# Reordering the first-batch attention head of a fused attention and mixture kernel

## Chip, cores and metric

The kernel runs on one core of one Trainium2 chip. The metric is the device time of one launch in microseconds (us). The kernel before the change takes 359.23 us, the median of five runs that lie between 359.01 and 359.6 us.

Five engines work side by side, each through its own instructions in order. PE is TensorE, the matrix engine; a matmul is preceded by a load of its weights, which the profile lists as PEld. DVE is VectorE, ACT is ScalarE, POOL is GpSimd and SP is SyncE. Engines wait for one another through semaphores. Matmul results go to PSUM, an accumulator memory that this kernel uses in eight banks of 512 fp32 numbers per partition; DVE and ACT copy them from there to SBUF, the working memory.

## What is computed

The reference is an attention in blocks whose keys and values are first mixed by a normalized 8 x 8 matrix, followed by a mixture of four two-layer networks.

```python
def _attn_ref(q, k, v, sort_net):          # q, k, v: 4 x 8 heads x 768 x 64
    P = sort_net
    for _ in range(5):
        P = P - np.max(P, axis=-1, keepdims=True)
        P = np.exp(P)
        P = P / (np.sum(P, axis=-1, keepdims=True) + 1e-09)
        P = P / (np.sum(P, axis=-2, keepdims=True) + 1e-09)
    k_sorted = np.einsum('bhij,bhjcd->bhicd', P, k_b).reshape(B, H, S, D)
    v_sorted = np.einsum('bhij,bhjcd->bhicd', P, v_b).reshape(B, H, S, D)
...
    scores = scale * np.matmul(q_b, k_sb.transpose(0, 1, 2, 4, 3))
    attn = softmax(scores)
    return np.matmul(attn, v_sb)

def _moe_ref(x, domain_probs, w1, w2):     # x: 3072 x 512; w1: 4 x 512 x 1024
    p = domain_probs / (domain_probs.sum(-1, keepdims=True) + 1e-09)
    for e in range(E):
        h = np.maximum(x @ w1[e], 0.0)
        out += p[:, e:e + 1] * (h @ w2[e])
    return out
```

The listing is shortened: reshapes and type casts are left out, and the softmax is written as one word.

## The kernel before

The order of all work is written out by hand: the kernel is built under a manual schedule, so each engine's instructions stand in the order of the calls. The head is the stretch from the start to the first full-width layers. It loads batch 0, normalizes the 8 x 8 matrices, and takes batch 0 through attention and the first network without a trip through DRAM, so that PE has dense work soon.

Batch 0's eight heads are treated as two quads of four heads, `qd` 0 and 1. Blocks of 96 tokens come in pairs `qq`: pair 0 and pair 1 are what this change touches. For a quad and a pair the steps are these.

- `mix_half` (L485) multiplies keys or values by the mixing matrices: 24 matmuls of 64 columns at L495 into one PSUM tile. `mixed` (L503) casts two of the tile's four blocks to SBUF (L506), into `kT` for keys or `vT0` for values.
- `h_w` (L517) transposes the mixed values on PE (four matmuls at L522 for two blocks). Its copy to SBUF (L527) can be handed back as a function and called later.
- `h_s` (L540) forms the scores of a pair, eight matmuls at L550, and ACT exponentiates them (L556) into `ET`.
- `h_a` (L561) multiplies `ET` by the values, eight matmuls at L567. DVE then takes reciprocals of the sums (L578) and scales the result (L579) into `xsl`.
- `h_x` (L584) transposes `xsl` with a permutation, four matmuls at L592, and a copy (L596) puts it into `xT`, the input of the first layer.
- `group0` (L660) is the first layer of network 0 on 192 tokens, eight matmuls at L673 for half of the contraction. `[0, 1]` is quad 0's and `[2, 3]` is quad 1's half of it. Its result goes through ACT (L686).
- `keep_warm` (L478) issues matmuls on a constant whose result nobody reads.

In what follows a letter with two digits names such a step: s01 is the scores of quad 0 and pair 1, w its value transposes, a its product with the values, x its transposition, g a part of the first layer, mv1 the 24 matmuls that mix quad 1's values.

PSUM is divided into two pools, `psM` and `psA`, of two tiles each; a tile spans two banks. Scores fill the first 384 numbers of each bank of their tile. `side` (L536) gives the last 128 numbers of each bank, seen as 16-bit numbers, as the place for value transposes. `tails` is the same for the mixing tiles. So transposes often share both banks of a tile with scores or with mixed values.

The order around the change is L1372 to L1411. PE's order from L1376 on is: a00, mv1, s10, w01, x00, w10, s01, four keep-warm matmuls, a10, g for quad 0, w11, x10, a01, g, s11, g for quad 1, x01, g, a11. The transposes w01 are written to the side of `ps_s01` ahead of the scores s01 that share its banks. ACT's order over the same stretch is: exponential of s00, cast of `kT` of quad 0, two casts of `kT` of quad 1, first cast of mv1, exponential of s10, copy of x00, second cast of mv1, exponential of s01, copy of w01, copy of x10. DVE's is: casts of quad 0's values, normalization of a00, copy of w10, normalization of a10, one step of the token weights (L237, followed on SP by small DMAs at L241 to L226), normalization of a01, copy of w11.

Of the kernel before, what the change touches and what calls it, by code (L numbers as in the profile page):

```python
# [9 lines left out]
F32 = mybir.dt.float32  # L10
F16 = mybir.dt.float16
AF = mybir.ActivationFunctionType
ALU = mybir.AluOpType
# [4 lines left out]
def kernel(  # L18
# [11 lines left out]
    nc = tc.nc  # L30

    B, H, S, D = q.shape
    GH = B * H
    NB = sort_net.shape[-1]
    BLK = S // NB
# [3 lines left out]
    P = 128  # L39
# [7 lines left out]
    HB = NB // 2  # L47
    VW = D + 2
# [12 lines left out]
    att = ctx.enter_context(tc.tile_pool(name="att", bufs=2))  # L61
# [3 lines left out]
    state = {"n": 0, "q": 0}  # L65

    def psa(shape, dtype, name):
        state["n"] += 1
        return psA.tile(shape, dtype, tag="ps", name=name)

    def psm(shape, dtype, name):
        return psM.tile(shape, dtype, tag="ps", name=name)
# [50 lines left out]
    def head(b, nm, h):  # L123
        return natural[(b, nm, h // 4)][:, h % 4, :, :]
# [231 lines left out]
    vec, act = nc.vector.tensor_copy, nc.scalar.copy  # L356
# [118 lines left out]
    xsls0, xsl0 = {}, {}  # L475
    vT0 = {qd: from_spare(S) for qd in range(2)}

    def keep_warm(ps, n):  # L478

        for _ in range(n):  # L480
            nc.tensor.matmul(ps, dummy, dummy, start=True, stop=True)
# [3 lines left out]
    def mix_half(nm, qd, hf, pool, warm_up=0):  # L485

        ps = pool([P, 1024], F32, f"ps_m{nm}_{qd}_{hf}")
        keep_warm(ps[:, 0:P], warm_up)
        tails[(nm, qd, hf)] = ps[:, 2 * R * 64:1024].bitcast(F16).rearrange("p (n x) -> p n x", n=2)
        ps = ps[:, 0:2 * R * 64].rearrange("p (s r x) -> p s r x", s=2, r=R)  # L490
        for sg in range(2):
            for r in range(R):
                for hh in range(2):
                    h = 4 * qd + 2 * sg + hh
                    nc.tensor.matmul(  # L495
                        ps[ds(D * hh, D), sg, r, :],
                        head(0, nm, h)[:, r, :],
                        PI0[hf][:, h, :, :].rearrange("p i c -> p (i c)"),
                        start=True, stop=True,
                    )  # L500
        return ps

    def mixed(nm, qd, ps, i0, n, copy):  # L503

        dst = kTs[qd][:, 0:S] if nm == "k" else vT0[qd]
        copy(  # L506
            dst.rearrange("p (i x c) -> p x i c", i=HB, c=CP)[:, :, ds(i0, n)],
            ps.rearrange("p s r (i c) -> p (s r) i c", c=CP)[:, :, ds(i0, n)],
        )
# [7 lines left out]
    def h_w(qd, copy, i0=0, n=HB, at=None):  # L517

        ps = psa([P, n, 2 * P], F16, f"ps_w_{state['n']}") if at is None else at
        for m in range(n):  # L520
            for sg in range(2):
                nc.tensor.transpose(  # L522
                    ps[0:BLK, m, ds(sg * P, P)], vT0[qd][:, ds((2 * (i0 + m) + sg) * BLK, BLK)], ident[:]
                )

        def evacuate(copy):
            copy(  # L527
                vs0s[qd][:, ds(i0, n), :, :, 0:D].rearrange("c i s h d -> c i (s h) d"),
                ps[0:BLK].rearrange("c i (x d) -> c i x d", d=D),
            )  # L530

        if copy is None:
            return evacuate
        evacuate(copy)

    def side(ps):  # L536

        return ps[:, :, 384:512].bitcast(F16)

    def h_s(qd, qq, ps=None):  # L540

        kT, ET = kTs[qd], ETs[2 * qd + qq % 2]
        if ps is None:
            ps = psa([P, 2, 512], F32, f"ps_s0_{qd}_{qq}")
        for n in range(4):
            for hh in range(2):
                sg, i = n // 2, 2 * (qq % 2) + n % 2

                m = BLK if 2 * i + sg == 3 else P
                nc.tensor.matmul(  # L550
                    ps[0:m, hh, ds(n * BLK, BLK)],
                    kT[ds(D * hh, D), ds((2 * i + sg) * BLK, m)],
                    qT0[qd][ds(D * hh, D), sg, qq // 2, :, ds((2 * (qq % 2) + n % 2) * CP, CP)],
                    start=True, stop=True,
                )
        nc.scalar.activation(  # L556
            ET[:, 0:S].rearrange("c (h x) -> c h x", h=2), ps[0:BLK, :, 0:HS],
            AF.Exp, bias=0.0, scale=SCALE,
        )

    def h_a(qd, qq, ps=None):  # L561
        ET = ETs[2 * qd + qq % 2]
        if ps is None:
            ps = psa([P, 2, 512], F32, f"ps_a0_{qd}_{qq}")
        for hh in range(2):
            for n in range(4):
                nc.tensor.matmul(  # L567
                    ps[:, hh, ds(n * VW, D + 1)],
                    ET[:, ds((4 * hh + n) * BLK, P)],
                    vs0s[qd][:, 2 * (qq % 2) + n % 2, n // 2, hh, 0:D + 1],  # L570
                    start=True, stop=True,
                )
        if qq not in xsls0:
            xsls0[qq] = att.tile([P, 2, 4, 2, D], F16, name=f"xsl0_{qq}", tag="xsl")[0:BLK]
        xsl = xsl0[(qd, qq)] = xsls0[qq][:, qd]
        av = ps[0:BLK, :, 0:4 * VW].rearrange("c h (n w) -> c h n w", w=VW)
        rz = att.tile([BLK, 2, HB, 1], F32, name=f"rz_{state['n']}", tag="rz", bufs=4)
        nc.vector.reciprocal(rz[:], av[:, :, :, D:D + 1])  # L578
        nc.vector.tensor_tensor(  # L579
            xsl.rearrange("c n h d -> c h n d"), av[:, :, :, 0:D],  # L580
            rz[:].broadcast_to([BLK, 2, 4, D]), ALU.mult,
        )

    def h_x(qq, copy, qds=range(2), ps=None, warm_up=0):  # L584

        nq = len(qds)
        if ps is None:
            ps = psa([P, 2, 512], F32, f"ps_x0_{qq}_{qds[0]}")
        keep_warm(ps[:, 0, 0:P], warm_up)
        for m, qd in enumerate(qds):  # L590
            for n in range(4):
                nc.tensor.matmul(  # L592
                    ps[:, m, ds(n * BLK, BLK)], xsl0[(qd, qq)][:, n, :, :].rearrange("c h d -> c (h d)"),
                    perm[:], start=True, stop=True,
                )
        copy(  # L596
            xTs[0][:, :, ds(2 * qq, 2), :].rearrange("p (q s) i x -> p q s (i x)", q=2)[:, ds(qds[0], nq)],
            ps[:, 0:nq, 0:4 * BLK].rearrange("p q (s x) -> p q s x", s=2),
        )
# [374 lines left out]
    for e in range(E):  # L974
        w, hk, hf = w1sb[e], NKC // 2, FF // 2
# [396 lines left out]
    mk1 = mix_half("k", 1, 0, psm)  # L1372
    mixed("k", 1, mk1, 0, 2, act)
    mixed("k", 1, mk1, 2, 2, act)
    ps_a00, ps_s10 = [psa([P, 2, 512], F32, f"ps_{n}") for n in ("a00", "s10")]
    h_a(0, 0, ps_a00)  # L1376
    mv1 = mix_half("v", 1, 0, psm)
    mixed("v", 1, mv1, 0, 2, act)
    h_s(1, 0, ps_s10)
    ps_s01 = psm([P, 2, 512], F32, "ps_s01")  # L1380
    w01 = h_w(0, None, 2, 2, side(ps_s01))
    h_x(0, act, [0], ps_a00)
    h_w(1, vec, 0, 2, tails[("v", 1, 0)])
    mixed("v", 1, mv1, 2, 2, act)
    h_s(0, 1, ps_s01)
    w01(act)
    ps_a10 = psa([P, 2, 512], F32, "ps_a10")
    keep_warm(ps_a10[:, 0, 0:P], 4)
    h_a(1, 0, ps_a10)
    next(p_steps)  # L1390
    group0(0, 1, 0, [0, 1])
    ps_a01 = psa([P, 2, 512], F32, "ps_a01")
    w11 = h_w(1, None, 2, 2, side(ps_a01))
    h_x(0, act, [1], ps_a10)
    h_a(0, 1, ps_a01)
    w11(vec)
    group0(0, 1, 1, [0, 1])
    ps_s11 = psa([P, 2, 512], F32, "ps_s11")
    h_s(1, 1, ps_s11)
    evacuate00 = group0(0, 1, 0, [2, 3], True)  # L1400
    h_x(1, act, [0], ps_a01)
    evacuate00()
    group0(0, 1, 1, [2, 3])
    h_a(1, 1, ps_s11)
# [17 lines left out]
    def builds(b):  # L1422
# [10 lines left out]
    later = [  # L1433
        [(h_q, 1, 1, vec)],
        [(h_v, 1, 1, act)],
        [(h_s, 0, 2), (h_w, 1, vec)],
        [(h_w, 0, vec), (h_s, 1, 2)],
        [(h_a, 0, 2)],
        [(h_s, 0, 3), (h_a, 1, 2)],
        [(h_s, 1, 3), (h_a, 0, 3)],  # L1440
        [(h_x, 2, act), (h_a, 1, 3)],
# [30 lines left out]
    for g in range(G0 + 1):  # L1472
        b, c = divmod(g, R // 2)
# [56 lines left out]
```

## Time and profile before

The profile is one execution with its own device time. All rows below come from it.

| What | us |
|---|---|
| median of five runs | 359.23 |
| the profiled execution's own time | 359.23 |
| its span, first to last instruction | 357.4 |
| so outside the span | 1.83 |
| PE busy in 0 to 11.80 | 8.84 |
| PE busy in 11.80 to 18.46 | 6.16 of 6.66 |
| PE busy in 18.46 to 36.88 | 18.42 of 18.42 |
| PE busy in 36.88 to 357.40 | 316.99 of 320.52 |

Busy times are unions of the recorded spans of an engine's instructions. Matmuls overlap in the pipeline, so a matmul's recorded end lies after the start of the next one; the distance from the start of one group to the start of the next is what the group costs PE when nothing waits. A timeline row gives the start, the length from the group's first start to its last end, the engine, the line, the output and inputs, and the number of instructions; a bracket at its end names the idle time before it and what ended it. The granted TensorE clock was 1.00 in all four stretches.

### The profile page before, as it was taken

The page shows a single profiled execution, that of the slowest core. Times are in us where ns is not written, and L with a number is a line of the kernel's source. Part 1 is how long each engine was busy: PE and PEld are TensorE (multiplying, and loading weights), DVE is VectorE, ACT ScalarE, POOL GpSimd, SP SyncE. Part 2 cuts the span into 40 slices and gives each one's busy share as a digit, 9 for nine tenths or more (in the row PEclk, how much of TensorE's full clock was granted, in tenths as well). Part 3 has the DMA queues.
Part 4 walks back from the last instruction along what each step waited for, and adds up shares of the span by engine and source line. Part 5 has one row for each costly group of instructions (what it writes and reads, how often), then busy time and mean ns, then how long its engine had stood idle before and what let it go on. Part 6 is the DMA issues. An engine that isn't in the chain of part 4 may idle for free.

```text
span 357.4 us, 9499 instructions
## 1 busy us (share of the span) xinstructions
PE 350.4 (98%) x3949; PEld 305.3 (85%) x3949; DVE 275.4 (77%) x550; ACT 171.5 (48%) x305; POOL 133.6 (37%) x149
## 2 busy tenths in 40 slices
PE   8799999999999999999999999999999999999996
PEld 8686857888888888888899888888888888888885
DVE  5754897769888587778889978896588876688963
ACT  2664330442424445368947158820388511688201
POOL 8873010365122420000626318840068800288400
PEclk9999999999999999999999999999999999999999
DMA  8999999999999999745994410005200014100011
GB/s 117 208 207 229 214 209 198 205 187 178 196 176 175 213 90 196 142 87 69 176 208 67 115 65 0 2 2 136 91 11 2 3 54 124 61 0 2 2 73 47
DMA packets 72023, 40.52 MB, mean 113 GB/s; under 512 B 40614, under 2 KB 66732, under 8 KB 71980
## 3 DMA queue, kind: packets, MB, share of 16 engines
q0 software_dynamic: 36576, 19.93, 41.4%
q1 hardware_dynamic: 35260, 19.92, 27.4%
q8 instruction: 31, 0.51, 0.6%
q14 instruction: 12, 0.10, 0.1%
q10 hardware_dynamic: 144, 0.07, 0.1%
HBM read 42.13 MB, written 6.34 MB: 136 GB/s over the span
## 4 chain that ended last, share of the span: by engine, by line
PE 95%; DVE 2%; ACT 1%; DMA 0%; issue 0%
PE ps_h L784 18%; PE ps_Q L1258 18%; PE ps_p L768 12%; PE ps_X L1115 10%; PE ps_Z L1115 7%; PE ps_Q L1115 7%; PE ps_Z L1258 6%; PE ps_h L673 3%; PE ps_o L708 3%; PE ps_p L824 3%; PE ps_a L453 2%; PE ps_s L418 2%; PE ps_k L399 1%; PE ps_v L365 1%; PE ps_mk L495 1%; PE ps_s L550 0%
## 5 line engine op out<-in xcount | busy, mean ns | idle before, releaser
L784 PE MATMUL ps_h<-xT,w 128*128 128x256 f16 x576 | 67.5, 273 | 0.0
L784 PEld LDWEIGHTS <-w 128*128 128x128 f16 x576 | 55.2, 98 | 7.2
L790 DVE SCALAR_TENSOR_TENSOR Hb<-ps_h,pb 128x1024 f16<-128x1024 f32 x34 | 41.5, 1223 | 17.3 <-PE ps_h L784 16.6
L1115 PEld LDWEIGHTS <-w 128*128 128x128 f16 x480 | 43.6, 98 | 4.8
L1128 POOL TENSOR_TENSOR arena<-tmp,pb 128x512 f16<-128x512 f32 x12 | 15.2, 1274 | 65.7 <-PE ps_Z L1115 49.8
L1258 PEld LDWEIGHTS <-Hb 128*128 128x128 f16 x320 | 31.1, 98 | 3.5
L1127 ACT ACTIVATE tmp<-tmp 128x512 f32<-128x512 f32 x46 | 29.0, 632 | 3.9 <-DVE tmp L1165 3.9
L1258 PEld LDWEIGHTS <-Sb 128*128 128x128 f16 x304 | 28.2, 98 | 3.0
L1115 PEld LDWEIGHTS <-arena 128*128 128x128 f16 x312 | 27.7, 98 | 2.9
L425 ACT ACTIVATE ET<-ps_s 96x768 f16<-96x768 f32 x24 | 18.1, 802 | 25.1 <-PE ps_s L418 24.8
L408 ACT CAST kT<-ps_k 64x384 f16<-64x384 f32 x48 | 22.7, 474 | 13.3 <-PE ps_k L399 12.3
L121 POOL DMA_DIRECT2D arena<-in_q_dram x24 | 19.9, 844 | 14.8 <-DMA q_ring<-arena 14.8
L1115 PE MATMUL ps_X<-ET,arena 128*128 128x256 f16 x168 | 25.2, 272 | 0.0
L1258 PE MATMUL ps_Q<-w,Hb 128*128 128x256 f16 x192 | 24.6, 273 | 0.0
L768 PEld LDWEIGHTS <-Hb 128*128 128x128 f16 x232 | 21.8, 98 | 3.0
L1121 DVE SCALAR_TENSOR_TENSOR Hb<-ps_X,pb 128x512 f16<-128x512 f32 x27 | 18.7, 692 | 7.0 <-PE ps_X L1115 7.0
L1135 ACT COPY ps_X<-ps_Z 128x512 f32<-128x512 f32 x27 | 15.4, 571 | 17.8 <-PE ps_Z L1115 17.8
L1115 PE MATMUL ps_Z<-xT,w 128*128 128x256 f16 (+1 forms) x176 | 22.5, 258 | 0.0
L754 DVE TENSOR_TENSOR Sb<-Hb 128x512 f16<-128x512 f16 x33 | 20.6, 647 | 0.0
L1142 ACT COPY tmp<-ps_X 128x512 f32<-128x512 f32 x26 | 15.2, 586 | 9.2 <-PE ps_X L1115 6.6
L1121 DVE SCALAR_TENSOR_TENSOR Hb<-ps_Z,pb 128x512 f16<-128x512 f32 x27 | 18.4, 683 | 1.3 <-PE ps_Z L1115 1.3
L1165 DVE TENSOR_TENSOR tmp<-ps_Q,tmp 128x512 f32<-128x512 f32 x26 | 17.8, 683 | 0.8 <-PE ps_Q L1115 0.8
(265 smaller groups left out, 739.7 us busy)
## 6 DMA issues: line engine op xcount, KB each, us to landing
w<-in_moe_w_dram POOLq DMA_DIRECT2D x6, 1024.0 KB, 28.0
pb<-p_dram SPq DMA_DIRECT2D x9, 512.0 KB, 6.5
arena<-in_k_dram POOLq DMA_DIRECT2D x8, 384.0 KB, 7.6
arena<-in_v_dram POOLq DMA_DIRECT2D x8, 384.0 KB, 7.6
vs<-arena SPq DMA_DIRECT2D x36, 66.0 KB, 5.0
arena<-in_q_dram POOLq DMA_DIRECT2D x24, 96.0 KB, 6.3
out_dram<-ob SPq DMA_DIRECT2D x9, 256.0 KB, 2.1
w<-in_moe_w_dram POOLq DMA_DIRECT2D x4, 512.0 KB, 11.9
```

The lines of the kernel that those rows point to most:

```text
L121: nc.gpsimd.dma_start(t[:, h // 2, :, h % 2, :], q[b, h].rearrange("(t p) d -> p t d", p=P))
L408: nc.scalar.copy(kT[ds(D * hh, D), r], pk[ds(D * r, D), hh].rearrange("p a (i c) -> p a i c", c=CP),)
L425: nc.scalar.activation(ETs[2 * (pr % 2) + hh][:, 0:S].rearrange("c (a x) -> c a x", a=2), pss[hh][0:BLK, :, 0:HS], AF.Exp, bias=0.0, scale ...
L754: tt(sm[0], blk(0, 1), blk(1, 1), ALU.add)
L768: nc.tensor.matmul(ps, lhs(e, f), Ts[e][rhs][:, f, :], start=(first and e == es[0] and f == 0), stop=(done and e == es[-1] and f == KH - 1 ...
L784: nc.tensor.matmul(ps[:, f, :], w1sb[e][:, kc, ds((4 * g + f) * P, P)], xT[:, kc, ds(2 * c * P, 2 * P)], start=(kc == 0), stop=(kc == NKC ...
L790: nc.vector.scalar_tensor_tensor(out=Hb[:, homes.get(e, e), ds(4 * g, 4), :], in0=ps[:], scalar=0.0, op0=ALU.max, in1=weights(e).broadcast ...
L1115: nc.tensor.matmul(dst[:, ds(f * cols, cols)], a[lhs][:, k, ds((f0 + f) * P, P)], t[rhs][:, k, :], start=(first and f == 0 and k == 0), st ...
L1121: nc.vector.scalar_tensor_tensor(out=home(i, j), in0=src.rearrange("p (f x) -> p f x", f=m), scalar=0.0, op0=ALU.max, in1=weight(j).broadc ...
L1127: nc.scalar.activation(src, src, AF.Relu, bias=0.0, scale=1.0)
L1165: tt(t12, Q, u2, ALU.add)
L1258: nc.tensor.matmul(ps, lhs(e, f), Ts[e][rhs][:, f, part], start=(first and e == 0 and f == 0), stop=(e == E - 1 and f == KH - 1), skip_gro ...
```

## The change

The head is reordered around the first values product. The scores s01 and the transposes w01 move from behind w10 and s10 to directly behind a00; in that move s01 comes ahead of w01, which writes to the side of the tile that s01 has just filled. `ps_s01` becomes a `psA` tile and `ps_s10` a `psM` tile. The first cast of mv1 and the copy of w01 go from ACT to DVE. x00 moves ahead of s10. The product a01 moves ahead of a10, so ahead of the first layer, and goes into `ps_s01` in place of a tile of its own; its normalization is held back (`later`) until x10 is issued. Two of four keep-warm matmuls are dropped. `ps_s11` reuses the tile of a10.

```diff
-    def h_a(qd, qq, ps=None):
+    def h_a(qd, qq, ps=None, later=False):
...
-        if qq not in xsls0:
-            xsls0[qq] = att.tile([P, 2, 4, 2, D], F16, name=f"xsl0_{qq}", tag="xsl")[0:BLK]
...
-        nc.vector.reciprocal(rz[:], av[:, :, :, D:D + 1])
...
+        def even():
+            if qq not in xsls0:
+                xsls0[qq] = att.tile([P, 2, 4, 2, D], F16, name=f"xsl0_{qq}", tag="xsl")[0:BLK]
...
+            nc.vector.reciprocal(rz[:], av[:, :, :, D:D + 1])
...
+        if later:
+            return even
+        even()
...
-    ps_a00, ps_s10 = [psa([P, 2, 512], F32, f"ps_{n}") for n in ("a00", "s10")]
+    ps_a00, ps_s01 = [psa([P, 2, 512], F32, f"ps_{n}") for n in ("a00", "s01")]
     h_a(0, 0, ps_a00)
+    h_s(0, 1, ps_s01)
+    w01 = h_w(0, None, 2, 2, side(ps_s01))
+    ps_s10 = psm([P, 2, 512], F32, "ps_s10")
     mv1 = mix_half("v", 1, 0, psm)
-    mixed("v", 1, mv1, 0, 2, act)
+    mixed("v", 1, mv1, 0, 2, vec)
+    w01(vec)
+    h_x(0, act, [0], ps_a00)
     h_s(1, 0, ps_s10)
-    ps_s01 = psm([P, 2, 512], F32, "ps_s01")
-    w01 = h_w(0, None, 2, 2, side(ps_s01))
-    h_x(0, act, [0], ps_a00)
     h_w(1, vec, 0, 2, tails[("v", 1, 0)])
     mixed("v", 1, mv1, 2, 2, act)
-    h_s(0, 1, ps_s01)
-    w01(act)
     ps_a10 = psa([P, 2, 512], F32, "ps_a10")
-    keep_warm(ps_a10[:, 0, 0:P], 4)
+    keep_warm(ps_a10[:, 0, 0:P], 2)
+    even01 = h_a(0, 1, ps_s01, True)
     h_a(1, 0, ps_a10)
     next(p_steps)
     group0(0, 1, 0, [0, 1])
-    ps_a01 = psa([P, 2, 512], F32, "ps_a01")
-    w11 = h_w(1, None, 2, 2, side(ps_a01))
+    w11 = h_w(1, None, 2, 2, side(ps_s01))
     h_x(0, act, [1], ps_a10)
-    h_a(0, 1, ps_a01)
+    even01()
     w11(vec)
     group0(0, 1, 1, [0, 1])
-    ps_s11 = psa([P, 2, 512], F32, "ps_s11")
+    ps_s11 = ps_a10
     h_s(1, 1, ps_s11)
     evacuate00 = group0(0, 1, 0, [2, 3], True)
-    h_x(1, act, [0], ps_a01)
+    h_x(1, act, [0], ps_s01)
     evacuate00()
     group0(0, 1, 1, [2, 3])
     h_a(1, 1, ps_s11)
```

PE's order becomes: a00, s01, w01, mv1, x00, s10, w10, two keep-warm matmuls, a01, a10, g, w11, x10, g, s11, g, x01, g, a11. ACT's: the casts of `kT`, exponential of s01, copy of x00, exponential of s10, second cast of mv1, copy of x10. DVE's: normalization of a00, first cast of mv1, copy of w01, copy of w10, normalization of a10, L237, normalization of a01, copy of w11. The order on POOL and SP is unchanged, and so is everything from a11 on.

More of the change, by code (lines that the diff above doesn't have):

```diff
@@ L572, in h_a @@
                 )
-        if qq not in xsls0:
-            xsls0[qq] = att.tile([P, 2, 4, 2, D], F16, name=f"xsl0_{qq}", tag="xsl")[0:BLK]
-        xsl = xsl0[(qd, qq)] = xsls0[qq][:, qd]
-        av = ps[0:BLK, :, 0:4 * VW].rearrange("c h (n w) -> c h n w", w=VW)
-        rz = att.tile([BLK, 2, HB, 1], F32, name=f"rz_{state['n']}", tag="rz", bufs=4)
-        nc.vector.reciprocal(rz[:], av[:, :, :, D:D + 1])
[L579 to L582, printed above, removed]
+        def even():
+            if qq not in xsls0:
+                xsls0[qq] = att.tile([P, 2, 4, 2, D], F16, name=f"xsl0_{qq}", tag="xsl")[0:BLK]
+            xsl = xsl0[(qd, qq)] = xsls0[qq][:, qd]
+            av = ps[0:BLK, :, 0:4 * VW].rearrange("c h (n w) -> c h n w", w=VW)
+            rz = att.tile([BLK, 2, HB, 1], F32, name=f"rz_{state['n']}", tag="rz", bufs=4)
+            nc.vector.reciprocal(rz[:], av[:, :, :, D:D + 1])
+            nc.vector.tensor_tensor(
+                xsl.rearrange("c n h d -> c h n d"), av[:, :, :, 0:D],
+                rz[:].broadcast_to([BLK, 2, 4, D]), ALU.mult,
+            )
+        if later:
+            return even
+        even()
     def h_x(qq, copy, qds=range(2), ps=None, warm_up=0):
```

## Prediction

> **What bounds the kernel.** I read the page's totals first, then who PE waited for, then the timeline of the head.
>
> ```profile
> span 357.4 us, 9499 instructions
> PE 350.4 (98%) x3949; PEld 305.3 (85%) x3949; DVE 275.4 (77%) x550; ACT 171.5 (48%) x305; POOL 133.6 (37%) x149
> PE 95%; DVE 2%; ACT 1%; DMA 0%; issue 0%
> ```
>
> The chain that ended last is PE for 95% of the span. The list of waits of PE over 0 to 30 us has four entries, and over 30 to 360 us it has none. So whatever the head gives PE late or early is carried whole to the end.
>
> ```profile
> PE ps_R L316 <- DVE sn L304: 1.9, 1, 1.9
> PE ps_w L260 <- DVE Hb L152: 1.1, 1, 1.1
> PE ps_s L550 <- ACT kT L506: 0.2, 1, 0.2
> PE ps_mk L495 <- DVE Rs L1366: 0.2, 1, 0.2
> ```
>
> All four lie ahead of a00. From the timeline, the stretch that the change reorders:
>
> ```profile
> 14.88 1.42 ACT L506 CAST kT<-ps_mk 128x384 f16<-128x384 f32 x3
> 15.12 0.55 DVE L506 CAST Sb<-ps_mv 128x384 f16<-128x384 f32 x1
> 15.34 0.42 PE L567 MATMUL ps_a<-Sb,ET 96*128 96x65 f16 x8
> 15.68 0.57 PE L495 MATMUL ps_mv<-Sb,arena 128*64 128x64 f16 x24
> 16.18 0.35 PE L550 MATMUL ps_s<-Sb,kT 64*128 64x96 f16 x8
> 16.29 0.48 ACT L506 CAST Sb<-ps_mv 128x384 f16<-128x384 f32 x1
> 16.46 0.42 PE L522 MATMUL ps_s<-ident,Sb 128*96 128x128 f16 x4
> 16.67 0.81 ACT L556 ACTIVATE ET<-ps_s 96x768 f16<-96x768 f32 x1
> 16.77 0.34 PE L592 MATMUL ps_a<-perm,xsl 96*128 96x96 f16 x4
> 16.95 0.39 PE L522 MATMUL ps_mv<-ident,Sb 128*96 128x128 f16 x4
> 17.27 0.34 PE L550 MATMUL ps_s<-Sb,kT 64*128 64x96 f16 x8
> 17.47 0.42 DVE L527 COPY Sb<-ps_mv 96x512 f16<-96x512 f16 x1 [0.76 <-ACT ET L556]
> 17.93 0.48 ACT L506 CAST Sb<-ps_mv 128x384 f16<-128x384 f32 x1
> 17.95 0.40 PE L567 MATMUL ps_a<-Sb,ET 96*128 96x65 f16 x8
> 18.46 0.82 PE L673 MATMUL ps_h<-xT,w 128*128 128x192 f16 x8
> 18.62 0.69 DVE L579 TENSOR_TENSOR xsl<-ps_a,rz 96x512 f16<-96x512 f32 x1
> 19.37 0.34 PE L592 MATMUL ps_a<-perm,xsl 96*128 96x96 f16 x4
> ```
>
> PE runs from group to group with hardly a hole: mv1 at 15.68, s10 at 16.18, w01 at 16.46, x00 at 16.77, w10 at 16.95, s01 at 17.27, keep-warm at 17.55, a10 at 17.95, g at 18.46. Other work hides the latencies: while ACT casts mv1 and DVE copies w10, PE does s10, w01, x00, s01 and keep-warm matmuls. The start-to-start distances are the costs below: mix 0.50, s 0.28, x 0.18, a 0.24, g 0.66. A change from s, a or x to full rows or back costs more: a00 to mv1 took 0.34, w10 to s01 0.32, and g to s11 0.76 (19.88 to 20.63). A waiting engine starts about 0.04 after PE's recorded end and 0.05 after ACT's or DVE's.
>
> **The change, step by step, on this execution's clock.** Up to a00 (15.34) nothing differs.
>
> *s01 ahead of mv1.* It needs the second cast of quad 0's values on DVE, which ends at 15.67. It is a wait on a separate instruction, like the one of the w10 copy (PE's end 17.34, copy 17.47: 0.14), so s01 starts at about 15.80, and its recorded end is 0.35 later, 16.15. ACT's second cast of quad 1's keys begins at 15.82 (the three casts end at 16.30, the last is 0.48 long); ACT starts its next instruction 0.38 after such a cast (16.29 to 16.67). Both give 16.19 for the exponential of s01. It takes 0.81: it ends at 17.00.
>
> *w01 behind s01.* This is the new wait. In the changed program's order the transposes w01 wait for the exponential of s01, because they write into the banks that it reads, though in other columns. Before, w01 came first and the scores filled the banks afterwards. PE could have begun w01 at 15.80 + 0.28 = 16.08; it begins at 17.05. Everything on PE queues behind: 0.97 us with nothing on PE. Nothing covers it, since mv1, x00 and s10, which were ready or could have been, stand behind it in PE's order.
>
> *The chain through quad 1's values.* w01 17.05 + 0.32 gives mv1 at 17.37, x00 at 17.87, s10 at 17.87 + 0.29 = 18.16 (x to s is not shown with no wait before it; 0.18 to 0.34 by the rows of x and of a to mv1). mv1's recorded end is 17.37 + 0.57 = 17.94. Its cast is on DVE now: 0.56 by the row of 13.63, in place of 0.48 on ACT; 17.98 to 18.54. w10 then starts at 18.59 (PE was free at 18.44: 0.15 lost). Its copy: 18.59 + 0.39 + 0.14 = 19.12, done at 19.54. The exponential of s10 is ready by then: s10 ends at 18.51, ACT is free from its x00 copy at 18.25 + 0.38 = 18.63, done 19.44. In the hole PE does two keep-warm matmuls and a01 (from 18.97, when DVE's copy of w01, 18.50 to 18.92, is done, to 19.21). a10 starts at 19.59, against 17.95: a hole of 0.38.
>
> *The first layer.* g directly behind a10 at 19.83. Before, it stood 0.51 behind a10, as it waited for ACT's second cast of mv1 (17.93 + 0.48 = 18.41); in the changed program it does not. Against 18.46 that is 1.37 late. w11 at 20.49. x10 needs xsl of a10: 19.59 + 0.40 + 0.04, reciprocal 0.24 to the next start, 0.69: 20.95, so x10 at 21.00; PE was free at 20.71, a hole of 0.29. Here a01 no longer stands between x10 and g, which saves 0.27 (19.64 minus 19.37) plus 0.24 (a01 itself) less the 0.18 of x10: 0.33. g at 21.18 against 19.88: 1.30 late. s11 at 21.18 + 0.76 = 21.94; ACT's copy of x10 is done at 21.86, just in time.
>
> *Behind it* the order is that of before, with the same distances. x01 at 22.9 needs the normalization of a01 and the copy of w11 on DVE, done by 22.4 (L237 0.31, reciprocal and product 0.93, copy 0.42, from 20.9 on). Two dropped keep-warm matmuls save 0.11, and it goes into holes. The copies moved off ACT cost nothing there: ACT was not on the chain. The token-weight DMAs follow L237, which goes from 19.23 to about 20.87; their first consumer on PE, at 30.20, moves by 1.30. The trace has the packets of the small load it reads in by 28.7, so 1.5 us of slack loses 0.34. POOL's and SP's queues are in the old order.
>
> Sum, by start times after less before: a10 +1.64 (holes 0.12 + 0.97 + 0.15 + 0.38, and 0.02 net of all that moved or went), from a10 to g -0.27 (0.24 in place of 0.51), from w11 to x10 +0.26 (0.51 in place of 0.25), from x10 to g -0.33: +1.30, and PE carries it to the end. Span 357.4 + 1.3 = 358.7; the profiled execution took 359.23, equal to the median of the five, so 359.23 + 1.30 = 360.53. The steps that have no row (x to s, wait instruction, w01 to mv1 after a hole) are good to 0.1 each: 1.0 to 1.6.
>
> The trace of before shows such a guard of shared banks: DVE's copy from the mixed-values tile ends at 17.89, and ACT's cast from other columns of the same tile starts at 17.93, though ACT was free for it from 17.75 (its x00 copy began at 17.37, plus 0.38). [...] If columns alone counted, w01 would start at 16.08, and the first rival below would hold.
>
> **The rivals.** *The guard does not cost its whole length.* Then w01 16.08, mv1 16.40, x00 16.90, s10 17.19, cast on DVE 17.01 to 17.57, w10 at 17.62, its copy done at 18.57, a10 18.62, x10 20.03, g 20.21: 0.33 late, 359.56. Even so no gain, because mv1 stands 0.7 later than before and a10 hangs on it through two copies. For it: the head's latencies could be shorter than I chain them. Against: the exponential is 0.81 in every row. Chance 0.10.
>
> *PE is fed through and the removed work comes out.* The change then pays: keep-warm 0.11, the 0.11 in which PE shows nothing before g, and some 0.1 of small waits of x10 and a01 go, PE has no new hole: -0.3, 358.9. It decides if the exponential of s01 and the copies of mv1 and w10 end before PE gets there, that is if w01 starts by 16.1 and a10 by 17.7. For it: those holes are in the trace, and PE's matmuls are otherwise the same. Against: a chain of mix, cast, transpose and copy after mv1 took 2.27 us (15.68 to 17.95), and mv1 starts later. To be faster by 0.7 it would need more than all waits behind a00. Chance 0.05.
>
> *More is lost downstream:* x01, or the token weights, come late as well; 0.3 to 0.6 on top, 361.0. Against: 0.4 and 1.1 us of slack in the steps above. Chance 0.05. A PE hole of one us could also lower the granted clock; the trace has a longer one, 1.9 us up to 11.79, behind which the clock stayed 1.00.
>
> **How the numbers follow.** The forecast, +1.0 to +1.6 with the guard, has chance 0.80: 360.53, own range 360.2 to 360.9. The range takes in the first rival's edge and the last rival: 359.6 to 361.1. About 0.2%, 0.72 us here, is what a measurement of this kernel tells from no change. The forecast is above that but for its low end; the first and second rival fall within. Slower 0.85, same 0.12, faster 0.03.
>
> **What would show it.** Right: in the profile after, PE waits for ACT's exponential (ET, L556) ahead of the transposes at L522, some 1.0 us, near 16 us; a10 near 19.6; g near 19.8; a11 near 23.7 against 22.41; the rest of the span the same length. Wrong: w01 right behind s01 with no hole, or the first g before 18.5, or later holes on PE that shrink.

## The result and the profile after

The changed kernel takes 360.70 us (median of 43 executions, 360.08 to 362.61) against 359.66 (median of 80, 358.94 to 361.82): a ratio of 1.0032, 95% interval 1.0023 to 1.0040. It is slower, by 1.04 us in the medians. Ratios leave out executions more than 1.5% above the fastest of their kernel, which matters only for the late loads below. The profiled execution took 360.17 us. Its page answers to the totals shown of before:

```profile
span 358.4 us, 9494 instructions
PE 351.1 (98%) x3947; PEld 305.8 (85%) x3947; DVE 276.3 (77%) x552; ACT 170.6 (48%) x303; POOL 133.5 (37%) x149
PE 94%; DVE 3%; ACT 1%; DMA 0%; issue 0%; DVEq 0%
```

PE is still the chain, and its share of that chain fell by one point. The list of waits of PE in 0 to 30 us (total, times, longest, all in us but the middle one) tells where:

```profile
PE ps_R L316 <- DVE sn L304: 1.3, 1, 1.3
PE ps_w L260 <- DVE Hb L152: 1.1, 1, 1.1
PE ps_s L522 <- ACT ET L556: 0.9, 1, 0.9
PE ps_a L567 <- DVE Sb L527: 0.2, 1, 0.2
PE ps_s L550 <- ACT kT L506: 0.2, 1, 0.2
PE ps_mk L495 <- DVE Rs L1372: 0.2, 1, 0.2
```

Third and fourth are new. The third is a transpose into `ps_s` that waits for ACT's exponential `ET`. Over 30 to 360 us the list is empty, as before. The timeline of the stretch (start, length, engine, line, work; idle time before it in brackets):

```profile
15.33 0.42 PE L567 MATMUL ps_a<-Sb,ET 96*128 96x65 f16 x8
15.81 0.34 PE L550 MATMUL ps_s<-Sb,kT 64*128 64x96 f16 x8
16.19 0.81 ACT L556 ACTIVATE ET<-ps_s 96x768 f16<-96x768 f32 x1
17.05 0.38 PE L522 MATMUL ps_s<-ident,Sb 128*96 128x128 f16 x4 [0.90 <-ACT ET L556]
17.37 0.57 PE L495 MATMUL ps_mv<-Sb,arena 128*64 128x64 f16 x24
17.98 0.56 DVE L506 CAST Sb<-ps_mv 128x384 f16<-128x384 f32 x1 [1.27 <-PE ps_mv L495]
18.59 0.42 PE L522 MATMUL ps_mv<-ident,Sb 128*96 128x128 f16 x4
19.12 0.42 DVE L527 COPY Sb<-ps_mv 96x512 f16<-96x512 f16 x1 [0.26 <-PE ps_mv L522]
19.59 0.40 PE L567 MATMUL ps_a<-Sb,ET 96*128 96x65 f16 x8 [0.23 <-DVE Sb L527]
19.83 0.82 PE L679 MATMUL ps_h<-xT,w 128*128 128x192 f16 x8
21.01 0.34 PE L598 MATMUL ps_a<-perm,xsl 96*128 96x96 f16 x4
21.19 0.82 PE L679 MATMUL ps_h<-xT,w 128*128 128x192 f16 x8
23.73 0.41 PE L567 MATMUL ps_a<-Sb,ET 96*128 96x65 f16 x8
```

From top to bottom: a00, s01, its exponential, w01 behind the hole, mv1 and its cast, w10 and its copy, a10, first g, x10, second g, a11. Each of these starts that the prediction named lies within 0.03 us of it. Before, the second g and a11 had these rows:

```profile
19.88 0.82 PE L673 MATMUL ps_h<-xT,w 128*128 128x192 f16 x8
22.41 0.41 PE L567 MATMUL ps_s<-Sb,ET 96*128 96x65 f16 x8
```

a11 starts 1.32 us later than before (23.73 against 22.41), and PE's last matmul 1.33 later (355.00 against 353.67): nothing is recovered in between. The span grew by only 1.0. From the last matmul's start to the end of the span it took about 3.4 us, against 3.7 before; the last store landed 1.6 us behind its issue, against 1.9.

### The profile page after: what moved, and what is told of

It is laid out like the page before. It is cut to its first block, busy times and chain, and to the rows that moved or that the text cites. A ratio compares the mean times of both kernels' runs of the same rounds, so it can differ in the third digit from the quotient of the medians.

```text
span 358.4 us, 9494 instructions
## 1 busy us (share of the span) xinstructions
PE 351.1 (98%) x3947; PEld 305.8 (85%) x3947; DVE 276.3 (77%) x552; ACT 170.6 (48%) x303; POOL 133.5 (37%) x149
## 4 chain that ended last, share of the span: by engine, by line
PE 94%; DVE 3%; ACT 1%; DMA 0%; issue 0%; DVEq 0%
PE ps_h L790 18%; PE ps_Q L1264 18%; PE ps_p L774 12%; PE ps_X L1121 10%; PE ps_Z L1121 7%; PE ps_Q L1121 7%; PE ps_Z L1264 6%; PE ps_o L714 3%; PE ps_h L679 3%; PE ps_p L830 3%; PE ps_a L453 2%; PE ps_s L418 2%; PE ps_k L399 1%; PE ps_v L365 1%; PE ps_mk L495 1%; PE ps_a L567 1%
## 5 line engine op out<-in xcount | busy, mean ns | idle before, releaser
L796 DVE SCALAR_TENSOR_TENSOR Hb<-ps_h,pb 128x1024 f16<-128x1024 f32 x34 | 41.5, 1223 | 17.3 <-PE ps_h L790 17.1
L425 ACT ACTIVATE ET<-ps_s 96x768 f16<-96x768 f32 x24 | 18.1, 802 | 25.0 <-PE ps_s L418 24.8
```

The costliest lines, as they stand in the source:

```text
L425: nc.scalar.activation(ETs[2 * (pr % 2) + hh][:, 0:S].rearrange("c (a x) -> c a x", a=2), pss[hh][0:BLK, :, 0:HS], AF.Exp, bias=0.0, scale ...
L796: nc.vector.scalar_tensor_tensor(out=Hb[:, homes.get(e, e), ds(4 * g, 4), :], in0=ps[:], scalar=0.0, op0=ALU.max, in1=weights(e).broadcast ...
```

## The experiments

Five questions: what the hole at w01 costs and what makes it; whether the dealt-out copies, the moved product and the dropped keep-warm matmuls matter; what the old order pays that the new one does not; whether the order pays where values arrive late; and why the median lies above the changed kernel's own profiled execution. Group names are those of the prediction. An experiment with an interval was timed in rounds; the others are one execution each.

### Transposes ahead of the scores that share their banks

```diff
     h_a(0, 0, ps_a00)
-    h_s(0, 1, ps_s01)
     w01 = h_w(0, None, 2, 2, side(ps_s01))
+    h_s(0, 1, ps_s01)
     ps_s10 = psm([P, 2, 512], F32, "ps_s10")
```

> The changed kernel with the transposes w01 issued ahead of the scores s01, as before the change; all else as changed. Theory (guard of shared banks, 0.97 us): no hole on PE at w01; by the rows w01 15.8, s01 16.1, mv1 16.4, w10 17.6, a10 18.6, second g 20.2, a11 22.8: 0.96 us less than the changed kernel, still 0.3 to 0.4 us more than before, since mv1 starts 0.7 us later than before. Rival (the loss is the late chain mv1, cast, w10, copy, a10, and PE's hole at w01 only lies in its shadow): a10 stays near 19.6, a11 near 23.7. Rival (fewer keep-warm matmuls, or casts on DVE): no change either.

Measured: 359.32 us (12 executions, 359.13 to 360.89), ratio to before 0.9991, interval 0.9977 to 1.0005. The hole is gone, and two waits for loads appear in its trace:

```profile
15.72 0.42 PE L522 MATMUL ps_s<-ident,Sb 128*96 128x128 f16 x4
16.08 0.34 PE L550 MATMUL ps_s<-Sb,kT 64*128 64x96 f16 x8
16.84 0.57 PE L495 MATMUL ps_mv<-Sb,arena 128*64 128x64 f16 x24 [0.41 <-DMA arena<-in_v_dram]
22.07 0.83 PE L679 MATMUL ps_h<-xT,w 128*128 128x192 f16 x8 [0.30 <-DMA w<-in_moe_w_dram]
23.57 0.41 PE L567 MATMUL ps_a<-Sb,ET 96*128 96x65 f16 x8
```

w01 and s01 follow each other. mv1 waits for the load of quad 1's values, which landed at 16.79 in this execution, and a later g waits for weights. So a11 came at 23.57 here and not at the expected 22.8: in this execution, which took 360.02 us and lies above the median, the loads took most of what the hole had taken. Over the 12 executions the exchange of two calls takes all of the loss back: the interval lies wholly below that of the changed kernel. Against the kernel before no difference can be told, but the expected 0.3 to 0.4 us more than before (a ratio of 1.0008 to 1.0011) lies outside the interval. What is missing there is taken up below.

### The same guard in the old order

```diff
     ps_s01 = psm([P, 2, 512], F32, "ps_s01")
+    h_s(0, 1, ps_s01)
     w01 = h_w(0, None, 2, 2, side(ps_s01))
     h_x(0, act, [0], ps_a00)
...
-    h_s(0, 1, ps_s01)
     w01(act)
```

This is the kernel before, with only s01 moved directly ahead of w01.

> The kernel before, with one edit: the scores s01 issued directly ahead of the transposes w01, where w01 stood, so that they share banks in the new order. Theory: w01 waits for the exponential of s01, which here stands behind that of s10 on ACT (17.37 to 18.18); w01 at 18.23, a hole of 1.5 us on PE; a10 19.6 and a11 24.0, 1.6 us later than before's 22.41. Rival (the late chain of quad 1 is the cause): mv1 starts at 15.68 as before, so at most 0.3 us (s01 ahead of w10).

Measured: 363.59 us in one execution. Its timeline has the hole at the predicted place:

```profile
18.38 0.38 PE L522 MATMUL ps_s<-ident,Sb 128*96 128x128 f16 x4 [1.53 <-ACT ET L556]
```

Scores ahead of the transposes in their own banks are enough to make the wait; nothing else of the change is needed. Up to a10 the size is as expected: 4.33 us behind a00, against 2.61 before. Behind a10 more is lost than expected: the granted clock was 0.50 from 19.8 to 23.2 us, just behind the hole, and a11 came at 25.49; a further wait of 1.0 us at L453, far behind the head, shows in this execution alone of those of the old order. This was the first sight of the clock, which is taken up below.

### Other banks, the same order

```diff
     h_s(0, 1, ps_s01)
-    w01 = h_w(0, None, 2, 2, side(ps_s01))
     ps_s10 = psm([P, 2, 512], F32, "ps_s10")
+    w01 = h_w(0, None, 2, 2, side(ps_s10))
     mv1 = mix_half("v", 1, 0, psm)
-    mixed("v", 1, mv1, 0, 2, vec)
     w01(vec)
+    mixed("v", 1, mv1, 0, 2, vec)
```

PE's order is that of the changed kernel; the transposes lie in the banks of another tile, and DVE copies them ahead of its cast of mv1.

> The changed kernel with PE's order untouched, but the transposes w01 go to the side of the tile of s10, which is free, and DVE copies them ahead of its cast of mv1. Theory: with other banks there is nothing to wait for; w01 16.08, mv1 16.4, w10 17.6, a10 18.6, a11 22.8, as with w01 first. Rival (the order s01, w01 itself, or the late chain, costs): a hole stays at w01, or a11 stays near 23.7.

Measured: 359.77 us in one execution. The head started 0.36 late here (a00 at 15.69), so the distances count:

```profile
16.17 0.35 PE L550 MATMUL ps_s<-Sb,kT 64*128 64x96 f16 x8
16.44 0.42 PE L522 MATMUL ps_s<-ident,Sb 128*96 128x128 f16 x4
16.80 0.57 PE L495 MATMUL ps_mv<-Sb,arena 128*64 128x64 f16 x24
```

w01 starts 0.28 behind s01, with no wait. The second g starts at 20.62: from a00 it is 4.93 us, against 5.86 in the changed kernel and 4.54 before. So the guard is worth 0.92 of the head's loss, and what is left, 0.40, is the price of the order without it: the first rival's chain, worked out as 0.33.

### The copies, the product, the keep-warm matmuls

Three edits, each on its own in the changed kernel. The first cast of mv1 back on ACT:

```diff
-    mixed("v", 1, mv1, 0, 2, vec)
+    mixed("v", 1, mv1, 0, 2, act)
```

> The changed kernel with the first cast of mv1 back on ACT; the copy of w01 stays on DVE. Theory: w10 starts 0.08 us earlier (18.51), but ACT now does the cast ahead of the x00 copy and the exponential of s10, which ends at 19.54 in place of 19.43; a10 stays at 19.6 and a11 at 23.7 within 0.05. Rival (the cast dealt to DVE is what costs): a11 0.1 to 0.3 us earlier.

Measured: 360.31 us in one execution. The cast takes 0.48 and w10 comes 0.08 earlier, but a10 stays at 19.60, and the engine it waits for has changed:

```profile
18.51 0.42 PE L522 MATMUL ps_mv<-ident,Sb 128*96 128x128 f16 x4
18.73 0.82 ACT L556 ACTIVATE ET<-ps_s 96x768 f16<-96x768 f32 x1
19.60 0.42 PE L567 MATMUL ps_a<-Sb,ET 96*128 96x65 f16 x8 [0.20 <-ACT ET L556]
```

On ACT the cast holds up the x00 copy and so the exponential of s10 (18.73 against 18.62). Both ways end at the same point, so the move of this cast is worth nothing here; the copy of w01 was not moved back on its own. Then the product a01 back behind x10:

```diff
-    even01 = h_a(0, 1, ps_s01, True)
     h_a(1, 0, ps_a10)
...
-    even01()
+    h_a(0, 1, ps_s01)
```

> The changed kernel with the product a01 back behind x10, its old place; the tile and all else as changed. Theory: in the changed kernel a01 fills a hole ahead of a10, for nothing, and is gone between x10 and g; back there it costs its 0.24 us again: a10 19.6 as changed, second g 21.43, a11 23.97. So this part of the change is a gain of 0.24 us. Rival (a01 ahead of a10 delays the first layer): a10 and the first g earlier by up to 0.24, a11 no later than 23.73.

Measured: 361.38 us in one execution, with the clock at 0.50 from 18.8 to 22.2. a01 stands between x10 and the second g again, but all of that stretch is stretched by the clock: its price can't be read from this run, and the 0.24 us expected of it are not shown. Last, no keep-warm matmuls:

```diff
-    keep_warm(ps_a10[:, 0, 0:P], 2)
```

> The changed kernel without its two keep-warm matmuls. Theory: they lie in a hole that ends with DVE's copy of w10; a10 19.6, a11 23.73 within 0.03, granted clock 1.00. Rival (dropping keep-warm matmuls lowers the clock or lets PE start late): matmul groups get longer, a11 later.

Measured: 360.29 us in one execution, a10 at 19.60 and a11 at 23.74, as in the changed kernel to 0.01. The two matmuls lie in a hole and cost nothing, and taking them out saved nothing.

### A small reorder of the kernel before

```diff
     w01 = h_w(0, None, 2, 2, side(ps_s01))
-    h_x(0, act, [0], ps_a00)
     h_w(1, vec, 0, 2, tails[("v", 1, 0)])
+    h_x(0, act, [0], ps_a00)
```

> The kernel before, with one edit: the transposes w10 ahead of x00. Theory: the chain mv1, cast, w10, copy, a10 bounds the head in the old order too; w10 at 16.82 in place of 16.95, a10 17.84 in place of 17.95, a11 22.29 in place of 22.41: 0.12 us less, 0.03 per cent, too little for the times to tell, to be read from the trace. Rival (PE is fed through in the old order and nothing but matmul time counts): a11 at 22.41 within 0.03.

Measured: 359.65 us (12 executions), ratio 0.9994, interval 0.9972 to 1.0017. From mv1 to a10 it took 2.18 in place of 2.27 us, so w10 does come to a10 sooner, by 0.08 us, which can't be told in the time. The trace also held something else: mv1 started at 15.90, since the values landed at 15.86. In the profile of before they had landed at 14.79.

### The kernel before once more, and the values late on purpose

The kernel before, unchanged, in another execution:

> The kernel before, unchanged, profiled once more. Theory: the profile of before is a lucky one for this load (14.79, the earliest of nine traces); here quad 1's values land later, and if they land after 15.63, PE shows a wait for this DMA at mv1, and a11 is later than 22.41 by about the same amount. Rival: a11 at 22.41 whatever the landing.

Measured: 359.55 us. The list of waits of PE has a line that the first profile of before did not have:

```profile
PE ps_mv L495 <- DMA arena<-in_v_dram: 0.5, 1, 0.5
```

The values landed at 16.21; mv1 started at 16.26 and a11 at 22.93, 0.52 later than in the profile that the prediction was read from. Then the load of quad 1's values was put behind the first half of the first layer's weights, in both kernels:

```diff
     load_natural(0, "k", 1)
+    load_w1(0, 2, [0])
     load_natural(0, "v", 1)
-    load_w1(0, 2)
+    load_w1(0, 2, [1])
```

In the kernel before:

> The kernel before with the load of quad 1's values put behind the first half of the first layer's weights, so that it lands some 2.5 us later (17.3 to 19.3 in place of the 14.8 to 16.8 seen in the traces so far). Theory added now (the old order needs these values at 15.68, the new one only at 17.37): PE waits for this load at mv1, and everything behind it shifts; with landing L, mv1 at L + 0.06, a10 2.27 later, the second g 4.20 after mv1. 1.7 to 3.5 us more than before. Rival (the load has slack in both orders): no change.

Measured: 364.29 us (8 executions, 362.05 to 369.20), ratio 1.0093, interval 1.0067 to 1.0120. Without three executions of 367.78 and more, which the ratio leaves out, the median is 363.81, 4.2 us more than before and above the expected 1.7 to 3.5: behind the wait the clock was 0.50 from 18.0 to 24.8 us in the profile, which the expectation did not have. The list of waits:

```profile
PE ps_mv L496 <- DMA arena<-in_v_dram: 2.9, 1, 2.9
```

In the changed kernel:

> The changed kernel with the same late load. Theory: the guard's hole (16.1 to 17.05) hides part of the wait; mv1 at L + 0.06 or 17.37, whichever is later, and the second g 3.82 after mv1 (17.37 to 21.19), so with the load as the bound the new order is 0.3 to 0.4 us faster than the old one with the same L: the sign of the change turns round. Rival (guard's hole adds to the wait for the load): still 1.0 to 1.3 us slower than the old order with the late load.

Measured: 362.56 us (6 executions, 362.26 to 368.74), ratio 1.0067, interval 1.0048 to 1.0087. Its profile is of the execution of 368.74, far above its median, so no sizes are read from it. With the late load the changed kernel is no longer the slower one. Without the execution of 368.74 its median is 362.55, 1.3 us below the 363.81 of the old order, but the two intervals overlap, so that it becomes the faster one is not settled. All 14 executions of the pair had a mean clock below 0.998, so the loss here is wait and clock together.

### The hole filled

```diff
     h_s(0, 1, ps_s01)
-    w01 = h_w(0, None, 2, 2, side(ps_s01))
     ps_s10 = psm([P, 2, 512], F32, "ps_s10")
+    keep_warm(ps_s10[:, 0, 0:P], 16)
+    w01 = h_w(0, None, 2, 2, side(ps_s01))
```

> The changed kernel with 16 small products of the identity in the hole between the second scores and the second weights' transposes; nothing reads their results. Theory: part of the changed kernel's median (about 0.4 of 1.04 us) is the granted clock, which was halved for one or two windows of 3.4 us in 15 of its 44 executions with a mean clock shown, because PE stood idle at the guard. With the hole filled the order of work stays (second weights' transposes near 17.05, a11 near 23.73 us), and almost no execution shows a mean clock below 0.998: median 360.2 to 360.3. Rival: the clock falls for another reason (the later waits of the head, or the chip): still about a third of the executions at 0.991 to 0.995 and a median of 360.7. A second rival, that the fillers themselves come between the scores and the exponential or run over into the transposes, would show as second weights' transposes later than 17.05 and a median above 360.7.

Measured: 360.73 us (11 executions, 360.11 to 362.00), ratio 1.0031, interval 1.0018 to 1.0045. The schedule held (w01 1.72 behind a00, as in the changed kernel), and one of 11 executions was below 0.998, as the theory had it. The median was not: 360.73 and not 360.2 to 360.3; the ten executions at 0.998 or more have 360.53, against 360.3 in the changed kernel, and why is open. The profiled execution, 361.24 at full clock, shows two delays that have nothing to do with the hole: a00 at 15.69, 0.36 late, and a wait near 180 us, far behind the head, at a line where only the old order with the guard had one too:

```profile
PE ps_a L453 <- DMA vs<-arena: 0.5, 1, 0.5
```

So this run speaks for the part on the clock, as far as one execution of 11 can, and not for its price in the median.

### The changed kernel once more

No edit.

> The changed kernel unchanged, once more. Theory (its hole at the guard leads to a halved clock in a part of the executions, wherever it runs): about a third of these executions, 2 to 6 of 11 or 12, show a mean granted clock of 0.991 to 0.995, the runs of before beside it at most one, and those at 0.998 or more have a median of about 360.3. Rival (the halved clock was a matter of where the earlier runs were made): none or one of these executions is below 0.998, and the filled hole has shown nothing. Both expect the profile of the changed kernel again: w01 1.72 us behind a00, a11 8.39 us behind a00, with no wait for the first quad-1 values as long as they land by 17.3 us.

Measured: 360.85 us (12 executions, 360.16 to 362.52), ratio 1.0026, interval 1.0008 to 1.0044. Five of the 12 were at 0.991 to 0.994; the other seven have a median of 360.34. Of the 17 executions of before beside it three were below 0.998 too, which is more than expected of them. The profiled execution, 361.05 us, is one of the five, and shows the halved clock in the changed kernel itself. The page's view by windows has, per stretch: length, busy time of PE, PEld, DVE, ACT, POOL with their instructions, the granted clock, the DMA share and GB/s:

```profile
13.90:17.30 3.40, 2.28 (x60) 1.98 (x57) 2.50 (x6) 2.74 (x5) 3.39 (x5) 1.00 1.14 213
17.40:20.80 3.40, 3.40 (x60) 3.06 (x60) 1.30 (x3) 1.73 (x3) 1.81 (x4) 0.50 1.21 205
```

And its timeline:

```profile
17.07 0.38 PE L522 MATMUL ps_s<-ident,Sb 128*96 128x128 f16 x4 [0.90 <-ACT ET L556]
17.38 0.85 PE L495 MATMUL ps_mv<-Sb,arena 128*64 128x64 f16 x24
18.17 0.50 PE L598 MATMUL ps_a<-perm,xsl 96*128 96x96 f16 x4
20.68 0.88 PE L679 MATMUL ps_h<-xT,w 128*128 128x192 f16 x8
```

Up to w01 it is the changed kernel's first profile to 0.02. Then the 24 matmuls of mv1, 0.50 from start to start before, take 0.79. The clock is back at 20.8. a11 starts 9.26 behind a00 and not 8.39, and this 0.87 goes through to the end (span 359.3 against 358.4).

## Why the prediction was right, and where it was not

*What bounds the kernel.* Held: PE, no waits of PE behind the head, and what the head loses the end has.

*w01 behind s01, "the new wait".* Held, place, releaser and size: 0.97 from where w01 could have begun, 0.90 of it recorded as idle behind s01's modelled end. Three runs show the cause: the hole goes when the transposes stand first, it goes when they lie in other banks, and it comes in the old order, 1.53 us long, when scores and transposes are exchanged.

*The chain through quad 1's values.* Held in every start. Two of its terms are real and yet not worth anything alone: the slower cast on DVE (0.56 us against 0.48 on ACT) is matched by a later exponential if the cast goes back, and the two keep-warm matmuls that remain lie in a hole.

*The first layer,* -0.27, +0.26 and -0.33: the starts of g, x10 and g agree to 0.02, so the sum does. The share of the moved product in the last term was not isolated.

*The first rival,* that the guard costs less than its length: wrong for this kernel. Its price, 0.33 late even with no hole, came out as 0.40 where the guard was taken away. *The second rival,* PE fed through, would have needed w01 by 16.1 and a10 by 17.7. With no hole a10 stood 3.34 behind a00, against 2.61 before: taking the guard away was not enough. *More lost downstream:* no wait of PE from 30 us on, so the head's timeline does not have it.

*The sum.* The forecast was 360.53, the median is 360.70. The schedule's +1.30 is +1.33 on PE. (Its own low end, +1.0, lies above the 0.72 that it names, so that end too could be told from no change.) But the number is near the median by terms that partly cancel, and three were missing or wrong.

First, the base. The prediction took one execution of before, equal to the median of the five shown, as typical. Its load of quad 1's values was the earliest seen: in twelve traces with the load in its usual place it landed between 14.79 and 16.79 us. The old order needs it by about 15.64 (mv1 starts 0.04 behind the landing), and in six of the twelve it was later; by these landings the old order would wait 0.24 us on a mean over the twelve, an estimate. The new order wants mv1 only at 17.37, behind the guard's hole, and no landing was later than that. So the hole hides a wait that the old order would pay with half of these landings. Shown is the wait, in two traces of the old order (mv1 at 16.26 and 15.90 in place of 15.68); its share in the medians is an estimate from the landings.

Second, the end: 3.4 to 3.5 us from the last matmul's start to the end of the span in eight traces of the new order, 3.6 to 3.9 in four of the old. Why the last store is quicker was not tried. These two terms, 0.24 and about 0.3, would also explain why the exchange of two calls came out no slower than before, though it keeps the longer chain of 0.33.

Third, the clock. The step that failed is this: "A PE hole of one us could also lower the granted clock; the trace has a longer one, 1.9 us up to 11.79, behind which the clock stayed 1.00." Behind the hole of 0.90 it did not stay 1.00, in a part of the executions. Of 56 recorded executions of the changed kernel 20 had a mean clock of 0.991 to 0.995, and a median of 361.38; the other 36 have 360.32. Of the 80 executions of before that were timed beside the experiments (not the 80 of the result, whose clocks are not on record), 4 were below 0.998, and the other 76 have 359.65. So at full clock the change costs 0.67, and the remaining 0.37 of the 1.04 lies with the executions in which the clock was halved. That the forecast of 360.53 lies so near the median is luck in this part: the profiled execution at full clock took 360.17, the median at full clock is 360.32, and only the halved clock, which the sum put at nothing, brings it to 360.70. From 13.9 to 17.3 the profiles have PE busy

| kernel | PE busy of 3.40 us | executions below 0.998 |
|---|---|---|
| before, first profile | 3.24 | 4 of 80 |
| hole filled | 3.03 | 1 of 11 |
| transposes first | 2.73 | 0 of 12 |
| changed | 2.28 | 20 of 56 |

Between the changed kernel and the one with the transposes first, 20 of 56 against 0 of 12 is hardly chance (1 in 100 if they were alike). With the hole filled, 1 of 11 points the same way but could be chance (8 in 100). These sets were not timed side by side, though; where the changed kernel and the kernel before were, 5 of 12 against 3 of 17 could be chance too (16 in 100). So that the hole brings on the halved clock is likely, and not shown beyond doubt.

Low PE busy in 3.4 us is not enough for it. In the changed kernel's second profile the 3.4 us ahead of the stretch with the hole had less work on PE than that stretch itself, and the clock behind them stayed 1.00:

```profile
10.60:14.00 3.40, 1.97 (x68) 1.76 (x68) 2.19 (x6) 1.06 (x2) 2.88 (x4) 1.00 1.30 201
14.00:17.40 3.40, 2.28 (x62) 1.90 (x56) 2.40 (x6) 2.74 (x5) 3.39 (x5) 1.00 1.13 212
```

In the profile of before PE was busy for only 1.50 of the 3.40 us from 8.40 to 11.80, and the clock behind them was 1.00 as well.

What picks the executions is open: the two profiles of the changed kernel have the same 2.28, and one kept its clock. In the second profile the clock is 0.50 from 17.39 to 20.80, for 3.41 us. In the same trace PE's first matmuls are slower up to 3.73 us (10 in the 0.70 us ahead of that point, 15 in the 0.70 us behind it; the clock column has 1.00 on both sides, so it does not show these first microseconds). From there to the halved stretch it is 13.66 us, four times 3.41, and with the product moved back it is 13.65 (5.12 to 18.77). Whether that is more than chance two traces do not tell, and together with PE's busy time it does not decide the clock either. Counted in steps of 3.41 us from that point, the halved stretch follows one with PE busy for 2.28 us (14.00 to 17.40). The changed kernel's first profile, with slower matmuls up to 5.41, has 2.35 from 15.64 to 19.05, with the hole inside, and behind it the clock was 1.00. The one with the cast on ACT has 2.28 to 2.53 in each of seven stretches of 3.40 us between 13.40 and 19.80, and its clock was 1.00 from 15 to 40 us.

## What to carry to other kernels

If matmuls of two kinds share a PSUM bank, issue those that nothing slow reads first: behind scores, a transpose into the same banks waits for the whole exponential (0.90 us here, or 1.53 in the old order), and exchanging two calls took it away. Before one execution is taken as the base of a sum of tenths, look at when its loads landed: a wait that this trace lacks may be one that many executions pay. And do not take a clock that held behind a longer hole in one trace (1.9 us here) as proof that a shorter one (0.90) is safe: look at the mean clock of many executions.

## What was not expected of the hardware

The landing of one and the same load, issued at 5.5 us in the same program place, spread over 2.0 us (14.79 to 16.79) in twelve traces. Some 1.1 us of idle PE or more within 3.4 us were followed by a clock of 0.50 for 3.4 us in the traces of three kernels (the changed one, the product moved back, and the old order with the guard, where PE was busy for 1.49 of 3.40), and for 6.8 us, 18.0 to 24.8, behind the 2.9 us wait for late values. As much idle time or more was also followed by a clock of 1.00: 1.43 of 3.40 us from 10.60 to 14.00 in the second profile of the changed kernel, 1.12 from 13.90 to 17.30 in its first, and 1.90 from 8.40 to 11.80 in the profile of before.
